# Attention head and FFT on one core: positions split 32 by 64, two filter pieces per TensorE visit

## The chip, the core and the metric

The kernel runs on one core of one Trainium2 chip. The metric is device time in microseconds (us), the median of three runs. The core's engines each follow their own list of instructions and wait for each other by semaphores: TensorE (PE in the profile, PEld for its weight loads), VectorE (DVE), ScalarE (ACT), GpSimd (POOL) and SyncE (SP). The last two mostly issue DMA transfers here.

## What is computed

Two independent results stand side by side in the output. `A` is attention with 16 query heads of 28 dimensions and one shared key and value head over 2048 positions. `B` is a filter in the frequency domain: a real two-dimensional FFT over positions (2048) and features (448), a product with a complex weight, and the way back.

```python
q = (x @ wq).reshape(B, S, H, Dh).transpose(0, 2, 1, 3)     # S 2048, H 16, Dh 28
k, v = x @ wk, x @ wv                                       # one head
p = softmax(einsum("bhqd,bkd->bhqk", q, k) * Dh ** -0.5)
a = einsum("bhqk,bkd->bhqd", p, v).transpose(0, 2, 1, 3).reshape(B, S, H * Dh) @ wo
X = rfft2(x_b, axes=(-2, -1)) * (w_r + 1j * w_i)            # 2048 x 225
b = irfft2(X, s=(S, D), axes=(-2, -1))
out = concatenate([a, b], axis=-1)
```

## The kernel before

The program has a head, a main loop and an end.

**Head.** The queries are projected in 16 groups: four chunks `c` of 512 positions by four groups `g` of 128 columns. Keys and values ride along in spare columns of the query weights. Numbers are split into a rounded part and a remainder (`xh`, `xl`, `wqh`, `wql`), so a group takes 11 matmuls (`proj`, line 367). ScalarE evacuates the result from PSUM into `qraw` and VectorE reduces its largest absolute value (`evac`, lines 371 and 372). The groups of chunks 1 to 3 are counted `n` = 0 to 11 below, group `n` being chunk `1 + n // 4`.

Between the groups stands the first stage of the filter's FFT. The 2048 positions of `B` come in eight pieces `q` of 256. For each piece VectorE folds the features (`fft1_fold`, lines 133 to 142: eight additions and subtractions, the first two over the halves of the 64 positions of a column, which makes a first radix-2 step); TensorE transforms the features (`fft1_a`, line 158, 64 small matmuls, ScalarE evacuating to `a`); TensorE transforms along positions (`fft1_b`, line 177, 16 matmuls of 64 by 64); the result `bs` is evacuated by ScalarE (pieces 0 to 5) or VectorE (6 and 7) and stored by SyncE to the DRAM tensor `t1`. Positions are split 64 by 32: 64 in this stage, 32 in the second. One piece is handled per slot: `slots` names the groups `n` = 3, 5, 6, 8, 9, 10 behind which a piece's `fft1_a` stands, with the `fft1_b` of the piece before it. Pieces 6 and 7 follow the last group, and the last `fft1_b` stands in the main loop, as unit `F` of `PLAN`.

Behind the projections come the keys and values. `fetch` copies seven four-row strips of `qraw` into `kf` rows 0 to 27 for the keys (by SyncE, one half of the positions at a time) and seven into rows 32 to 59 for the values (by GpSimd). `keys(h)` casts a half of the keys into `ka` (line 284, by ScalarE for half 0, VectorE for half 1), takes the remainder `kl` (line 288), and three DMAs copy these to three other row groups of `ka` (line 290). Half 1 is made at the very end of the head. The values are turned by 16 TensorE transposes (line 509) into one PSUM bank, which VectorE copies to `vs` (line 512). Also in the head: the largest query and key norms give a bound on the scores (`key_max` line 387, `terms`, `shift` line 299, `cmax`, `bits`), and `build_q` makes the first query tile `qa`, whose four row groups are filled by VectorE, ScalarE, SyncE and GpSimd (`copy_q`, lines 211 to 214).

In the head TensorE follows the order of the code. VectorE and ScalarE are ordered by the framework's scheduler, by the code's order and what is ready, and `behind` pins a few instructions behind others.

**Main loop.** 256 steps: 16 query tiles of (chunk, group) by 16 key tiles of 128. Per step, four score matmuls (line 929), their exponentials on ScalarE (line 864; those with `k` or `e` in `PLAN` are kept apart, lines 935, 940 and 954), and the output matmuls with `vs` (line 875). `PLAN` spreads over these steps the rest of the filter: units `A` and `B` (second FFT stage, the product with the weights, and its way back), `Z` (the first stage's way back), and `W` (output projection). All engines' orders are written out there: a host-side count of clocks in the code decides where waiting VectorE work goes. The PSUM banks are taken from a queue `free`.

**End.** The last output projection, and a slow path under a condition that these inputs do not meet.

## Time and profile before

| | |
|---|---|
| median of three runs | 633.81 us (633.77 to 633.99) |
| the profiled execution | 634.43 us |
| its span, first to last instruction | 632.6 us |
| TensorE, weight loads, VectorE, ScalarE busy | 627.0, 377.8, 440.0, 547.3 us |
| first projection behind the loads | 4.43 us |
| first score matmul (start of the main loop) | 69.22 us |
| granted TensorE clock | 1.000 |

All predicted times follow from the profiled execution's span; what lies outside it is 634.43 - 632.6 = 1.8 us. In a row of the timeline stand start, time taken, engine, line, operation, output and inputs, sizes, and how many equal instructions were merged. A matmul's record runs from its start to its modelled end, longer than the distance to the next start.

### The profile page before, as it was taken

How to read it: one execution, taken by the hardware profiler on the slowest of the kernel's cores; microseconds unless marked ns; L12 is line 12 of the kernel's file. 1: busy time of each engine (PE TensorE's matmuls, PEld its weight loads, DVE VectorE, ACT ScalarE, POOL GpSimd, SP SyncE). 2: the span in 40 equal slices, each digit the busy share in tenths (PEclk: the TensorE clock that was granted, in tenths of full speed). 3: DMA queues.
4: the chain of work that ended last, by engine and by line, in shares of the span. 5: the costliest groups of instructions: out<-in, count | busy, mean ns of one | idle time of the engine just before them, and what ended most of it. 6: DMA issues, size and time to landing. Idle time of an engine off the chain costs nothing. (4 is left out here: it accounts for less than half of the span.)

```text
span 632.6 us, 12167 instructions
## 1 busy us (share of the span) xinstructions
PE 627.0 (99%) x4436; PEld 377.8 (60%) x4436; DVE 440.0 (70%) x792; ACT 547.3 (87%) x985; POOL 61.2 (10%) x118
## 2 busy tenths in 40 slices
PE   9999999999999999999999999999999999999997
PEld 7877645656565655746555665565566565555555
DVE  5999648779999943866766845277687764467653
ACT  5655999999999998988889989999989989989992
POOL 3021311011213110000110100001010100000000
PEclk9999999999999999999999999999999999999999
DMA  8865773446456623226340413034152413030011
GB/s 249 295 175 163 235 173 99 115 132 180 121 152 144 155 59 74 67 65 187 77 106 18 125 36 82 16 83 147 35 129 60 105 53 88 16 82 11 20 31 61
DMA packets 37891, 66.74 MB, mean 106 GB/s; under 512 B 8009, under 2 KB 22746, under 8 KB 36860
## 3 DMA queue, kind: packets, MB, share of 16 engines
q1 hardware_dynamic: 32608, 52.50, 29.8%
q0 software_dynamic: 4640, 12.48, 7.9%
q8 instruction: 36, 0.59, 0.4%
q10 hardware_dynamic: 576, 0.92, 0.4%
q14 instruction: 31, 0.25, 0.1%
HBM read 29.81 MB, written 17.87 MB: 75 GB/s over the span
## 5 line engine op out<-in xcount | busy, mean ns | idle before, releaser
L864 ACT ACTIVATE p<-s 128x512 f32<-128x512 f32 x392 | 216.6, 636 | 24.9 <-PE s L929 23.9
L929 PE MATMUL s<-qa,ka 128*128 128x512 f32 x736 | 222.4, 402 | 0.0
L929 PEld LDWEIGHTS s<-qa,ka 128*128 128x128 f32 x736 | 134.7, 188 | 58.1 <-issue 26.0
L875 PE MATMUL s<-p,vs 128*32 128x512 f32 x1144 | 141.6, 595 | 0.0
L935 DVE COPY k<-s 128x512 f32<-128x512 f32 x119 | 78.2, 685 | 68.6 <-PE s L929 68.3
L954 ACT ACTIVATE k<-k 128x1024 f32<-128x1024 f32 x80 | 83.4, 1140 | 0.0
L864 ACT ACTIVATE qraw<-s 128x512 f32<-128x512 f32 x136 | 78.0, 648 | 2.3 <-PE s L929 2.3
L875 PEld LDWEIGHTS s<-p,vs 128*32 128x32 f32 x1144 | 34.5, 109 | 75.9 <-issue 69.1
L864 ACT ACTIVATE p<-po 128x512 f32<-128x512 f32 x88 | 56.0, 636 | 6.5 <-PE po L929 6.5
L929 PE MATMUL po<-qa,ka 128*128 128x512 f32 x151 | 60.9, 404 | 0.0
L929 PE MATMUL sx<-qa,ka 128*128 128x512 f32 x137 | 55.2, 403 | 0.0
L875 PE MATMUL s<-qraw,vs 128*32 128x512 f32 x424 | 54.8, 594 | 0.0
L875 PE MATMUL s<-k,vs 128*32 128x512 f32 x352 | 46.0, 594 | 0.0
L864 ACT ACTIVATE p<-sx 128x512 f32<-128x512 f32 x64 | 41.3, 645 | 3.0 <-PE sx L929 2.9
L749 POOL DMA_DIRECT2D ol<-ol x36 | 18.0, 507 | 228.0 <-DVE ol L772 155.8
L879 DVE STREAM_TRANSPOSE osb<-s 128x512 f32<-128x512 f32 x15 | 10.7, 716 | 38.9 <-PE s L875 38.8
L929 PEld LDWEIGHTS po<-qa,ka 128*128 128x128 f32 x151 | 28.4, 188 | 13.5 <-issue 6.7
L929 PEld LDWEIGHTS sx<-qa,ka 128*128 128x128 f32 x137 | 25.8, 188 | 11.0 <-issue 4.2
L875 PEld LDWEIGHTS s<-qraw,vs 128*32 128x32 f32 x424 | 13.2, 110 | 29.9 <-issue 28.7
L875 PEld LDWEIGHTS s<-k,vs 128*32 128x32 f32 x352 | 10.8, 110 | 24.9 <-issue 24.6
L864 ACT ACTIVATE qraw<-sx 128x512 f32<-128x512 f32 x35 | 22.7, 649 | 2.0 <-PE sx L929 2.0
L935 DVE COPY p<-s 128x512 f32<-128x512 f32 x37 | 24.1, 682 | 0.0
(263 smaller groups left out, 936.4 us busy)
## 6 DMA issues: line engine op xcount, KB each, us to landing
qa<-qa SPq DMA_DIRECT2D x15, 512.0 KB
raw<-xa SPq DMA_DIRECT2D x16, 256.0 KB
xb<-xb SPq DMA_DIRECT2D x8, 512.0 KB
qa<-qh SPq DMA_DIRECT2D x64, 64.0 KB
qa<-ql SPq DMA_DIRECT2D x60, 64.0 KB
t<-bs SPq DMA_DIRECT2D x16, 225.0 KB
wr<-wr POOLq DMA_DIRECT2D x16, 225.0 KB, 4.0
wi<-wi POOLq DMA_DIRECT2D x16, 225.0 KB, 5.2
```

Of the source, the lines that this page charges most:

```text
L749: nc.gpsimd.dma_start(ol[c][o, g].bitcast(F32), ol[c][r, 0].bitcast(F32))
L864: nc.scalar.activation(tiles[-1][:, h % 2], sc, AF.Exp, scale=SCALE)
L875: mm(po[c, g][32 * i:32 * i + 32], vs[:, kc], ps[i // 2][:, i % 2], start=(n == 1), stop=(n == 16))
L879: nc.vector.transpose(o, po[c, g])
L929: begun.append(mm(sc, ka[:, kc * 128:(kc + 1) * 128], qa[c, g][:, h], start=True, stop=True))
L935: nc.vector.tensor_copy(keep[i][h // 2][:, h % 2], sc)
L954: nc.scalar.activation(p, p, AF.Exp, scale=SCALE)
```

## The change

Seven parts, all but the last two in the head:

1. **Positions are split 32 by 64.** The first FFT stage transforms 32 positions, the second 64. The fold loses its first two instructions (the step over halves) and ends in the tile it began in (`xb`), from which TensorE then reads; so a piece's `xb` is free for the next load only behind its `fft1_a`. `t1` is `[64, 64, DF]`, and a second-stage tile is loaded by two DMAs of 64 partitions instead of four of 32. The constants `fw`, `fi`, `g1`, `g2` and the order of the weights follow; the sizes of the matmuls stay.
2. **Two pieces per visit.** `slots` is gone. `fft1_a` and `fft1_b` take two pieces: `a(0, 1)` behind group 4; `b(0, 1)`, `a(2, 3)` behind 7; `b(2, 3)`, `a(4, 5)` behind 10; `b(4, 5)`, `a(6, 7)`, `b(6, 7)` behind 11.
3. **The last `fft1_b` moves from the main loop into the head** (`F` leaves `PLAN`).
4. **The values are transposed on VectorE.** GpSimd fetches 28 strips of 512 positions into `vt` (7 values by 4 rows for each chunk), and one VectorE transpose in 32 by 32 blocks writes `vs`. TensorE's transposes and the evacuation go.
5. **The positions of the keys are permuted** to fit this: a key tile of 128 now takes 32 positions from each of the four chunks. So each half of `keys` fills 64 columns of every key tile, and its three DMAs move pieces of 64 elements. Half 1 is made behind group 10's `b(2, 3)`, by ScalarE.
6. **VectorE's and ScalarE's order is written out** from group 4 on; most `behind` calls are gone.
7. The order of the first `free` banks differs, and the output is put together on the host by the new split.

```diff
@@ head @@
+            ctx.enter_context(tc.manual_schedule(engines={mybir.EngineType.DVE, mybir.EngineType.Activation}))
+            group(4)
+            fft1_a(0, 1)
+            fft1_fold(2)
+            fft1_fold(3)
+            parts_of(3)
+            for j in range(NK):
+                split_x(*xs[3], 3, j)
+            group(5)
+            keys(0)
+            group(6)
+            fft1_fold(4)
+            group(7)
+            for v in range(3):
+                fetch_v(range(7, 14), v)
+            fft1_b(0, 1)
+            fft1_a(2, 3)
+            fft1_fold(5)
+            group(8)
+            group(9)
+            fetch(range(7), halves[1])
+            nc.vector.tensor_reduce(qm, qmx[:, 0:2], axis=AX.X, op=ALU.max)
+            fft1_fold(6)
+            group(10)
+            terms(0, 1)
+            fft1_fold(7)
+            fetch_v(range(7, 12), 3)
+            fft1_b(2, 3)
+            keys(1)
+            fft1_a(4, 5)
+            shift(0, 1)
+            qf, qh, ql = build_q(0, 0, True)
+            group(11)
+            terms(1, NC)
...
+        fetch_v(range(12, 14), 3)
+        copy_q(0, 1, qf, ql, nc.scalar)
+        fft1_b(4, 5)
+        copy_q(1, 1, qf, ql, nc.scalar)
+        fft1_a(6, 7)
+        for i in (2, 3):
+            copy_q(i, 1, qf, ql, nc.scalar)
         shift(1, NC)
-        top = nc.vector.tensor_reduce(cmax, cvec, axis=AX.X, op=ALU.max)
+        nc.vector.tensor_reduce(cmax, cvec, axis=AX.X, op=ALU.max)
...
+        fft1_b(6, 7)
...
-        pv = bank().rearrange("p (b d) -> p b d", b=16)
-        for b in range(16):
-            nc.tensor.transpose(pv[:, b], kf[32:64, b * 128:(b + 1) * 128], ident[32:64, 32:64])
-        fft1_out(6, pb6, bound)
-        fft1_a_out(7, 1, pa7)
-        nc.vector.tensor_copy(vs, pv)
-        keys(1, nc.vector.tensor_copy)
+        nc.vector.transpose(vs.rearrange("p t d -> p (t d)"), vt)
@@ fft1_fold @@
-            f = ff[q] = fp.tile([113, 4, 4, 2, 32], F32, name="f", tag="wi")
-            xv = x.rearrange("p k (j h m) -> p k j h m", h=2, m=32)
-            for h, op in enumerate((ALU.add, ALU.subtract)):
-                nc.vector.tensor_tensor(f[:, :, :, h], xv[:, :, :, 0], xv[:, :, :, 1], op=op)
...
+        f = fp.tile([113, 4, 256], F32, name="f", tag="wi")
+        nc.vector.tensor_tensor(f[:, 0:2], x[:, 0::2], x[:, 1::2], op=ALU.add)
+        nc.vector.tensor_tensor(f[:, 2:4], x[:, 0::2], x[:, 1::2], op=ALU.subtract)
+        nc.vector.tensor_tensor(x[:, 0], f[:, 0], f[:, 1], op=ALU.add)
+        nc.vector.tensor_tensor(x[:, 1], f[:, 0], f[:, 1], op=ALU.subtract)
+        nc.vector.tensor_tensor(x[:, 2], f[:, 2], f[:, 3], op=ALU.subtract)
+        nc.vector.tensor_tensor(x[:, 3], f[:, 2], f[:, 3], op=ALU.add)
@@ keys @@
+            src = kf[:, hs].rearrange("p (s t j) -> p s t j", s=2, j=32)
+            high = ka[:32].rearrange("p (t s j) -> p s t j", s=NC, j=32)[:, 2 * h:2 * h + 2]
+            nc.scalar.activation(high, src, AF.Copy)
...
+            kt = ka.rearrange("p (t x) -> p t x", t=16)[:, :, 64 * h:64 * h + 64]
+            low = kl.rearrange("p (t x) -> p t x", t=16)
+            for p, src in ((1, kt[:32]), (2, low), (3, low)):
+                nc.sync.dma_start(kt[32 * p:32 * p + 32].bitcast(F32), src.bitcast(F32))
@@ second stage @@
-            for l in range(2):
-                p = (r * 2 + l) * 32
-                ld = b2["last", q] = nc.sync.dma_start(b[p:p + 32].bitcast(F32), t1v[r, l][:, 4 * q:4 * q + 4])
-                behind(ld, begun[-1])
+            ld = b2["last", q] = nc.sync.dma_start(b[64 * r:64 * r + 64].bitcast(F32), t1v[r][:, 4 * q:4 * q + 4])
+            behind(ld, begun[-1])
```

Where the order moves, rows of the programs tell more. First TensorE between two groups of projections. Before, behind group 8, it does the fourth piece's first pass (L158) and the third piece's second pass (L177):

```order
L367 MATMUL s_87<-xh,wql 128x512
L158 MATMUL s_88<-cs_259,f 32x113 x4
...
L158 MATMUL s_89<-cs_259,f 32x112 x4
L177 MATMUL pbb<-a,fw 64x225 x2
L177 MATMUL po<-a,fw 64x225 x2
...
L367 MATMUL s_90<-xh,wqh 128x512
```

After the change, behind group 7 (the names are PSUM banks, `pbb` and `po` two more of them; L172 is the second pass, L155 the first):

```order
L369 MATMUL s_88<-xh,wql 128x512
L172 MATMUL pbb<-a,fw 64x225 x2
L172 MATMUL po<-a,fw 64x225 x2
...
L172 MATMUL s_89<-a,fw 64x225 x2
L172 MATMUL s_90<-a,fw 64x225 x2
L155 MATMUL s_85<-cs_260,xb 32x113 x4
...
L155 MATMUL s_88<-cs_260,xb 32x112 x4
L369 MATMUL s_89<-xh,wqh 128x512
```

Two second passes come first and two first passes behind them, and the next projection stands behind all four. Next TensorE at the end of the head and the first scores. Before:

```order
L498 MATMUL s_90<-sel_292,cmax 1x4 x4
L158 MATMUL s_85<-cs_259,f 32x113 x4
...
L509 MATMUL s_87<-ident,kf 128x32 x16
L929 MATMUL s_90<-qa,ka 128x512
...
L929 MATMUL s_85<-qa,ka 128x512
L177 MATMUL pbb<-a,fw 64x225 x2
L177 MATMUL po<-a,fw 64x225 x2
...
L875 MATMUL s_88<-k,vs 32x512 x4
```

And after:

```order
L301 MATMUL s_89<-prod,blk 128x12
L172 MATMUL pbb<-a,fw 64x225 x2
...
L172 MATMUL s_86<-a,fw 64x225 x2
L503 MATMUL s_90<-sel_291,cmax 1x4 x4
L917 MATMUL s_89<-qa,ka 128x512
L917 MATMUL s_87<-qa,ka 128x512
L917 MATMUL s_88<-qa,ka 128x512
L917 MATMUL s_85<-qa,ka 128x512
...
L863 MATMUL s_88<-k,vs 32x512 x4
```

The transposes and the second pass behind the first scores are gone, and two second passes stand ahead of the bound's matmuls and the scores. Last VectorE ahead of the main loop. Before, from the bound's input on:

```order
L494 TENSOR_REDUCE cmax<-cvec 128x4
L213 CAST qa<-qh 32x512 x2
L499 TENSOR_REDUCE bits<-s_90 1x1
L213 CAST qa<-qh 32x512 x2
L187 COPY bs<-s_88 128x450
L187 COPY bs<-s_89 128x450
L512 COPY vs<-s_87 128x512
L287 CAST ka<-kf 32x1024
L288 TENSOR_TENSOR kl<-kf,ka 32x1024
L187 COPY bs<-pbb 128x450
L187 COPY bs<-po 128x450
```

And after:

```order
L288 TENSOR_TENSOR kl<-kf,ka 32x2x16x32
L302 COPY cvec<-s_87 128x4
L232 TENSOR_SCALAR ql<-qraw,mask,cvec 128x512
...
L205 CAST qa<-qh 32x512 x4
L302 COPY cvec<-s_89 128x4x3
L499 TENSOR_REDUCE cmax<-cvec 128x4
L182 COPY bs<-pbb 128x450
...
L182 COPY bs<-s_86 128x450
L504 TENSOR_REDUCE bits<-s_90 1x1
L505 STREAM_TRANSPOSE vs<-vt 128x512
```

The remainder of the keys' second half (`kl`) has moved ahead of the first query tile, the four evacuations of the last two pieces stand together, and the transpose of the values closes the list. In the main loop the rows of TensorE and ScalarE read as before, with other bank numbers.

More of the change, by code (lines that the diff above doesn't have):

```diff
@@ L160, in fft1_a_mm, with fft1_b @@
         return pa
[L162 to L167 removed]
+    def fft1_b(*qs):
+        for i, q in enumerate(qs):
+            fft1_out(q, fft1_mm(q, [pair_of(bank()) for _ in range(2)] if i else None))
+            fft1_load(q + 4, (1,))
     def fft1_mm(q, pb=None):
@@ L479, with group @@
-            fetched = fetch(range(12, 14), slice(1536, S), nc.gpsimd)
-        behind(copy_q(0, 1, qf, ql, nc.scalar), last)
-        for p in range(2):
-            last = fft1_a_out(6, p, fft1_a_mm(6, p))
+            def group(n):
+                c, g = 1 + n // 4, n % 4
+                pq = pq1[g] if c == 1 else bank()
+                for j in range(1 if c == 1 else 0, NK):
+                    proj(pq, *xs[c], g, j)
+                if n == 10:
+                    key_max()
+                evac(c, g, pq)
@@ new lines @@
+            for n in range(4):
+                group(n)
+                if n == 0:
+                    parts_of(2)
+                    for j in range(NK):
+                        split_x(*xs[2], 2, j)
+                        xr[3, j] = raw(t["xa"][3, :, j], nc.sync)
+                    fft1_fold(1)
+                if n == 1:
+                    fetch(range(7), halves[0])
+            ctx.enter_context(tc.manual_schedule(engines={mybir.EngineType.DVE, mybir.EngineType.Activation}))
+            group(4)
@@ L495 @@
-        pb6 = fft1_mm(6, [pair_of(bank()) for _ in range(2)])
+        nc.vector.tensor_reduce(cmax, cvec, axis=AX.X, op=ALU.max)
         pb3 = bank()
+        fft1_b(6, 7)
         for g in range(NG):
             mm(pb3[0:1, 4 * g:4 * g + 4], cmax[:, g:g + 1], sel4, start=True, stop=True)
-        bound = nc.vector.tensor_reduce(bits, pb3[0:1, 0:16], axis=AX.X, op=ALU.max)
-        for i in range(4):
-            behind(copy_q(i, 0, qf, qh, nc.vector), top if i < 2 else bound)
-        for p in range(2):
-            behind(copy_q(2 + p, 1, qf, ql, nc.scalar), last)
```

182 lines of the change are left out of this document (57 added, 125 removed).

## The prediction

> **What bounds the kernel now.** I read the page first, then the busy time by stretches, the waits, and the head's instructions in order of time.
>
> ```profile
> span 632.6 us, 12167 instructions
> PE 627.0 (99%) x4436; PEld 377.8 (60%) x4436; DVE 440.0 (70%) x792; ACT 547.3 (87%) x985; POOL 61.2 (10%) x118
> ```
>
> TensorE is busy all the time, but a matmul's record overlaps the next one's, so 99% proves little. What counts is the distance between starts. The next view gives the stretch, then the busy time of TensorE, its weight loads, VectorE and ScalarE.
>
> ```profile
> 40.00:50.00 10.00, 10.00 (x119) 7.71 (x112) 9.96 (x20) 5.19 (x10) 1.54 (x4) 1.00 0.60 163
> 69.00:80.00 11.00, 11.00 (x77) 6.02 (x79) 5.39 (x9) 10.18 (x21) 0.20 (x1) 1.00 0.78 242
> 80.00:90.00 10.00, 9.92 (x55) 5.55 (x48) 3.51 (x6) 10.00 (x22) 0.43 (x1) 1.00 0.59 140
> ```
>
> In the head VectorE is as full as TensorE (9.96 of 10); behind it, from 69 to 90, ScalarE is. The list of TensorE's own waits from 20 to 70 has one entry, the 0.25 for VectorE that stands in a row below. ScalarE's list from 69 to 96 has one too (us in total, times, longest):
>
> ```profile
> ACT k L940 <- PE s L929: 0.9, 1, 0.9
> ```
>
> So the head runs at TensorE's pace, and the first 26 us of the main loop at ScalarE's: after its wait for the first scores it waits for nothing. **The end of the head is the first score's start, at 69.22**, and what moves it moves the end.
>
> **The price of a visit.** A visit is FFT work between projections. The columns are start, time, engine, line, operation.
>
> ```profile
> 20.46 0.39 PE L367 MATMUL po<-xh,wqh 128*128 128x512 f32 x1
> 24.99 0.39 PE L367 MATMUL s<-xh,wql 128*128 128x512 f32 x1
> 25.31 1.76 PE L158 MATMUL s<-cs,f 113*32 113x113 f32 x64
> 27.00 0.50 PE L367 MATMUL s<-xh,wqh 128*128 128x512 f32 x1
> 33.91 0.41 PE L177 MATMUL pbb<-a,fw 64*64 64x225 f32 x2
> 34.34 0.36 PE L177 MATMUL pbb<-a,fw 64*64 64x225 f32 x2
> 34.53 0.36 PE L177 MATMUL pbb<-a,fw 64*64 64x225 f32 x2
> 34.83 0.50 PE L367 MATMUL s<-xh,wqh 128*128 128x512 f32 x1
> 35.17 0.40 PE L367 MATMUL s<-xl,wqh 128*128 128x512 f32 x1
> 56.01 0.50 PE L387 MATMUL s<-qm,sel 128*128 128x1 f32 x4
> 56.44 1.76 PE L158 MATMUL s<-cs,f 113*32 113x113 f32 x64
> ```
>
> And from the view of one line, the shortest, median and longest of A's matmuls in ns:
>
> ```profile
> L158 PE MATMUL s<-cs,f x512: 257/259/284, 25.3 to 67.9; 113*32 113x112 f32 x86, 113*32 113x113 f32 x85
> ```
>
> I call the two passes of the FFT's first stage A (line 158, 64 matmuls a piece) and B (line 177, 16 matmuls). Projections start 0.227 apart: 20 steps from 20.46 to 24.99 take 4.53. Into A takes 0.32 (24.99 to 25.31). A's 64 matmuls end at 25.31 + 1.76 = 27.07, the last of 0.26 starts at 26.81: 1.50 from first to last start, and 0.19 to what follows (27.00). They are 16 sets of four row groups, so a further A joins at the distance of two sets, 1.50/15 = 0.10. B has its last pair at 34.55, 0.02 behind the row of 34.53, so it runs 0.64 from 33.91; a further B joins at 0.19 (34.34, 34.53); to a projection it takes 0.28. The first projection behind a visit takes 0.34 rather than 0.227 (34.83, 35.17), and those behind it a hundredth more for a while: I add 0.15 a visit. Not in the trace: projection to B (I take A's 0.32; the ends are 0.19, as from A, and 0.43, as from a score in the rows below, 69.22 + 2.24 - 0.50 = 70.96 to 71.39), and B to A (0.28, as to a projection; ends 0.19 and 0.32).
>
> **The head after, from 24.99.** Group 4: 11 projections, 2.50. Visit 1 (A, A): 0.32 + 1.50 + 0.10 + 1.50 + 0.19 = 3.61. Groups 5 to 7: 32 x 0.227 + 0.15 = 7.41. Visit 2 (B, B, A, A): 0.32 + (0.64 + 0.19 + 0.64) + 0.28 + 3.10 + 0.19 = 5.36. Groups 8 to 10: 7.41. Visit 3: the same 5.36; the key maximum makes 0.32 into 0.65 (one projection's 0.22 before it, 0.43 from 56.01 to 56.44); the shift adds 0.32. That is 6.01. Group 11: 10 x 0.227 + 0.15 = 2.42. For the last visit the rows of before are:
>
> ```profile
> 64.70 0.39 PE L299 MATMUL s<-prod,blk 128*128 128x12 f32 x2
> 65.02 0.99 PE L177 MATMUL s<-a,fw 64*64 64x225 f32 x16
> 66.26 0.32 PE L498 MATMUL s<-sel,cmax 128*1 128x4 f32 x7 [0.25 <-DVE cmax L494]
> 68.11 1.18 PE L509 MATMUL s<-ident,kf 32*128 32x32 f32 x16
> 69.22 2.24 PE L929 MATMUL s<-qa,ka 128*128 128x512 f32 x8
> 71.39 0.41 PE L177 MATMUL pbb<-a,fw 64*64 64x225 f32 x2
> 72.31 1.06 PE L875 MATMUL s<-k,vs 128*32 128x512 f32 x8
> ```
>
> After, it is visit 2's 5.36, the shift 0.32 (64.70 to 65.02), two more B 1.47, 0.28 out, the bound's matmuls 0.18, 0.15 to the score: 7.76. The transposes (68.11 to 69.22) are gone, and the wait at 66.26 is covered by the two B. The sum is 2.50 + 3.61 + 7.41 + 5.36 + 7.41 + 6.01 + 2.42 + 7.76 = 42.48, and **the first score starts at 67.47 instead of 69.22: 1.75 earlier**. In parts: transposes -1.1, wait -0.3, last B moved in +0.8, junctions the rest, some -1.1. With the unseen junctions at their ends it is 67.1 to 67.8.
>
> **The last B leaves the main loop** (0.92, 71.39 to 72.31). I cost that at nothing:
>
> ```profile
> 69.82 4.03 ACT L940 ACTIVATE k<-s 128x512 f32<-128x512 f32 x8 [0.94 <-PE s L929]
> 73.84 0.60 ACT L864 ACTIVATE p<-s 128x512 f32<-128x512 f32 x1
> ```
>
> ScalarE takes 4.03 for the first eight scores and goes on without a gap; its order there is unchanged, so it comes 1.75 earlier and no more. TensorE would reach the next scores earlier and wait. If TensorE were the limit there, it would be another 0.9.
>
> **Do the operands come in time?** VectorE loses two of eight instructions per fold. Groups of instructions, with busy time, mean ns and idle time before them:
>
> ```profile
> L133 DVE TENSOR_TENSOR f<-xb 113x512 f32<-113x512 f32 x14 | 9.1, 681 | 0.0
> 67.93 1.13 DVE L187 COPY bs<-s 128x450 f32<-128x450 f32 x2
> L371 ACT ACTIVATE qraw<-s 128x512 f32<-128x512 f32 x9 | 5.4, 598 | 11.9 <-PE s L367 11.9
> L372 DVE TENSOR_REDUCE qmx<-qraw 128x1 f32<-128x512 f32 x11 | 7.5, 678 | 0.0
> ```
>
> Per fold two of 0.6 to 0.68 go (four of the long form become two), 10 us over eight folds. That pays for the written order. There VectorE stands at the reduction of group 9 until its last projection (24.99 + 2.50 + 3.61 + 7.41 + 5.36 = 43.87, the start of group 8, + 5.0 = 48.9), its end (0.39) and its evacuation (0.6) are through, 49.9. Queued behind are that reduction (0.7) and folds 6 and 7 (2 x 2.6, with group 10's reduction and the first bound between them): done by about 56.7. TensorE wants fold 6 at visit 4's first A, 59.71 + 2.1 = 61.8. Cover 5 us; if it is gone, TensorE waits for the excess. The key maximum in visit 3 wants the reduction at 51.3: cover 0.7.
>
> Behind the first score: B 6 starts at 65.4, so VectorE's four copies run from 66.4 (0.57 each by the row, two in 1.13) to 68.7; the bound and the values' transpose, at the 716 of this row, end by 69.6:
>
> ```profile
> L879 DVE STREAM_TRANSPOSE osb<-s 128x512 f32<-128x512 f32 x15 | 10.7, 716 | 38.9 <-PE s L875 38.8
> ```
>
> The first output matmuls need four exponentials, 67.47 + 0.60 + 2.02 = 70.1. Cover 0.5. The fourth to sixth scores wait for banks until 68.1 to 68.9, ScalarE wants them from 69.6 on.
>
> **The keys** are the one new demand: key tiles now mix both halves of the keys, so the first score needs the second half, which before was needed only by the ninth tile.
>
> ```profile
> 55.32 4.57 SPq L281 DMA_DIRECT2D kf<-qraw  x7
> 78.44 1.77 SPq L599 DMA_DIRECT2D b<-t  x4
> 82.52 0.40 DVE L617 CAST bh<-b 128x450 fp32r<-128x450 f32 x1 [7.30 <-DMA b<-t]
> L284 ACT ACTIVATE ka<-kf 32x1024 fp32r<-32x1024 f32 x1 | 1.0, 1042 | 0.0
> L288 DVE TENSOR_TENSOR kl<-kf,ka 32x1024 fp32r<-32x1024 f32 x1 | 1.2, 1206 | 0.0
> wi<-wi POOLq DMA_DIRECT2D x16, 225.0 KB, 5.2
> qa<-ql POOLq DMA_DIRECT2D x4, 64.0 KB, 3.9
> L214 POOL DMA_DIRECT2D qa<-ql x4 | 2.0, 507 | 0.0
> ```
>
> SyncE has stores and loads of visit 2 ahead, long issued by then. Four of the seven fetches (4.57 for seven, 0.65 each) need group 8 alone, the last three leave by 49.9 + 2.0 = 51.9 and land 2.3 later (as the loads: issued by 80.21, used at 82.52), 54.2. ScalarE has the four evacuations of visit 3's B ahead (the last matmul of that B starts at 53.4, three more than 0.5 each behind it), until 55.0; the cast ends at 56.0. VectorE's low part, behind fold 7, ends at 57.9; its two issues behind the stores of visit 3 (some 0.65 each) end by 59.6. Landing 2.3 to 5.2 later: 61.9 to 64.8. Cover 2.7 us or more. In an unkind reading of the loads, whose 4 x 128 pieces took 4.1 in all, each key copy of 512 pieces takes 4.1 and they go one by one: 56.0 + 12.3 = 68.3, 0.8 late. I take the first, since the loads' 4.1 (78.44 to 82.52) is mostly issue (1.77) and landing (2.3). Behind the keys on SyncE four query copies issue until 62.2, and land by 67.4 even at 5.2. On POOL's queue a fetch of group 11's values (evacuated by 59.71 + 0.39 + 0.6 = 60.7) stands ahead of the other four: at 0.507 each they issue from 61.2 to 63.2, and at 3.9 the first lands at 65.1, the last, which the fourth score wants at 68.1, at 66.6. The last value fetch, behind them, lands by 67.6 at 3.9; the transpose starts at 68.9.
>
> The pieces of these copies are now 256 B, where they were 4096 B. No row has such a piece. The Trainium skill, "DMA: Bandwidth & Descriptors", Specifications, says that below 512 B a transfer leaves line rate, since the engine reads, modifies and writes; its section "Why small descriptors are slow (HBM only)" says that copies inside SBUF do not suffer so. By the second the sum above stands; the first is a rival, below.
>
> **The rivals.**
> - *TensorE limits the first scores after all*, and the last B counts too: 632.06 - 0.9 = 631.1. Against it: ScalarE's 10.18 and 10.00. Chance 0.12.
> - *Merging saves nothing*, because a visit's 0.32 and 0.28 are waits for ScalarE's evacuations, which merged visits meet again: then only transposes, wait and B are left, 1.75 - 1.1 = 0.65, 633.2. Against it: ScalarE stood idle for 11.9 us before its evacuations, waiting for TensorE (the row of line 371), not the other way round. Chance 0.10.
> - *The written order stalls*: an instruction that waits on VectorE or ScalarE holds all behind it, as the 7.30 at 82.52 shows. Some 1 us lost at the smallest covers (0.5 at the values' transpose, 0.7 at the key maximum) gives 633.0. Chance 0.18.
> - *Slower: the second half of the keys is late.* It costs from 67.47 on, makes the kernel slower by 0.2% from 69.22 + 1.27 = 70.5 on, which is at 4.8 us for each of the three copies, one by one. At twice the loads' 4.1, which is what the skill's 512 B rule would come to if it held here, 56.0 + 24.6 = 80.6: 11 us later than before, 645. Chance 0.07.
>
> **How the numbers follow.** The profiled execution took 634.43 with a span of 632.6; the median of the runs shown is 633.81, 0.62 less. 634.43 - 1.75 = 632.7 on that footing, 633.81 - 1.75 = 632.06 as a median. The forecast, 631.7 to 632.5, has 0.53. The range has to take in the first rival and most of the stalls: 630.8 to 633.4. Faster by over 0.2% (below 632.5, about what a measurement can tell): the forecast, the first rival and a little of the stalls, 0.69. Slower (above 635.1): the keys and the worst stalls, 0.08. The rest, 0.23, is the same.
>
> **What would show it.** Right: the first score near 67.5; three visits between projections, the second and third with no wait of TensorE; about 0.1 between two A of a visit; ScalarE's first exponential 0.6 behind the first score and no gap until some 24 us later; no L509 rows. Wrong: a wait of TensorE at the first score for key copies, at group 11 for folds or evacuations, or at the first output matmul for the values; or a main loop that is shorter or longer than 563.4 from first score to end by more than 0.5.

## The result, and the profile after

The changed kernel takes 632.50 us (median of 22 executions, 631.53 to 634.32) where the kernel before takes 634.25 on the same chips: a ratio of 0.9973, with a 95% interval of 0.9967 to 0.9979. That is 1.75 us or 0.27% faster; the prediction was 632.06 and 1.75 us. All ratios leave out executions in a disturbed state of the chip, which the cores' granted clocks show.

The page of the profiled execution (633.24 us) begins so:

```profile
span 631.5 us, 12130 instructions
PE 625.5 (99%) x4420; PEld 377.6 (60%) x4420; DVE 430.2 (68%) x775; ACT 547.2 (87%) x986; POOL 67.4 (11%) x132
```

VectorE has 9.8 us less to do than before (440.0), ScalarE the same (547.3). TensorE's rows in order of time show the visits (line 369 is a projection, 155 is A, 172 is B, 917 a score, 863 an output matmul):

```profile
25.61 0.39 PE L369 MATMUL s<-xh,wql 128*128 128x512 f32 x1
...
28.11 0.39 PE L369 MATMUL s<-xh,wql 128*128 128x512 f32 x1
28.43 3.30 PE L155 MATMUL s<-cs,xb 113*32 113x113 f32 x128
31.66 0.50 PE L369 MATMUL s<-xh,wqh 128*128 128x512 f32 x1
...
39.07 0.39 PE L369 MATMUL s<-xh,wql 128*128 128x512 f32 x1
...
40.20 0.94 PE L172 MATMUL s<-a,fw 64*64 64x225 f32 x16
41.07 3.30 PE L155 MATMUL s<-cs,xb 113*32 113x113 f32 x128
44.30 0.50 PE L369 MATMUL s<-xh,wqh 128*128 128x512 f32 x1
...
51.69 0.39 PE L369 MATMUL s<-xh,wql 128*128 128x512 f32 x1
...
57.50 0.48 PE L369 MATMUL s<-xh,wqh 128*128 128x512 f32 x1
...
59.88 0.39 PE L369 MATMUL s<-xh,wql 128*128 128x512 f32 x1
...
61.87 3.30 PE L155 MATMUL s<-cs,xb 113*32 113x113 f32 x128
...
66.04 0.41 PE L172 MATMUL pbb<-a,fw 64*64 64x225 f32 x2 [0.54 <-ACT a L144]
...
68.17 2.44 PE L917 MATMUL s<-qa,ka 128*128 128x512 f32 x8
70.53 1.39 PE L863 MATMUL s<-k,vs 128*32 128x512 f32 x8
```

A visit runs from the last projection ahead of it to the first behind it. This execution began 0.62 us later than that of before (the last projection of group 3 starts at 25.61, not 24.99), so distances are compared, not times:

| piece | predicted | measured |
|---|---|---|
| group 4 | 2.50 | 2.50 |
| visit 1 (28.11 to 31.66) | 3.61 | 3.55 |
| groups 5 to 7 | 7.41 | 7.41 |
| visit 2 (39.07 to 44.30) | 5.36 | 5.23 |
| groups 8 to 10 | 7.41 | 7.39 |
| visit 3 (51.69 to 57.50) | 6.01 | 5.81 |
| group 11 | 2.42 | 2.38 |
| visit 4 (59.88 to 68.17) | 7.76 | 8.29 |
| sum, from 25.61 to the first score | 42.48 | 42.56 |

Before, the same distance was 44.23: the head is 1.67 shorter. From the first score to the end it is 631.5 - 68.17 = 563.3, as before (563.4). ScalarE's start of the main loop and its only wait between 66 and 96:

```profile
68.76 4.03 ACT L928 ACTIVATE k<-s 128x512 f32<-128x512 f32 x8
72.60 0.68 ACT L852 ACTIVATE p<-s 128x512 f32<-128x512 f32 x1
```
```profile
ACT p L852 <- PE s L917: 0.5, 1, 0.5
```

TensorE's one new wait is the 0.54 at 66.04: the last visit's B waits for ScalarE's evacuation of the last A. TensorE's rows do not say why ScalarE was late. VectorE's and then ScalarE's rows do:

```profile
52.75 0.69 DVE L129 TENSOR_TENSOR f<-xb 113x512 f32<-113x512 f32 x1 [1.62 <-DMA xb<-xb]
...
58.96 1.21 DVE L288 TENSOR_TENSOR kl<-kf,ka 32x1024 fp32r<-32x1024 f32 x1
...
60.28 0.55 DVE L232 TENSOR_SCALAR ql<-qraw,mask,cvec 128x512 f32<-128x512 f32 x1
```
```profile
60.86 0.63 ACT L229 ACTIVATE qh<-ql 128x512 fp32r<-128x512 f32 x1 [2.41 <-DVE ql L232]
...
65.44 1.86 ACT L144 ACTIVATE a<-s 128x450 f32<-128x450 f32 x4
67.33 1.28 ACT L203 ACTIVATE qa<-ql 32x512 fp32r<-32x512 f32 x2
```

Fold 6 waits 1.62 for its piece of the input. SyncE's rows say when the load of a piece left, first before (piece 6), then after (pieces 6 and 7):

```profile
42.26 0.62 SPq L120 DMA_DIRECT2D xb<-xb  x1
```
```profile
46.93 1.10 SPq L120 DMA_DIRECT2D xb<-xb  x2
```

The buffer is now free only behind the first A of visit 2, which ends by 42.8 (half of the 3.30 that starts at 41.07, and its last matmul's end). The other 4 us lie in SyncE's own order, in which this load stands behind that visit's stores and small loads; no run here moves it ahead of them. Fold 7 and the low part of the keys stand behind fold 6 on VectorE, and the first query's shift (line 232) behind those. ScalarE comes to that query's cast in its written order and waits 2.41 for the shift, with the evacuation of group 11 and six more copies behind it. When the first score's result is there (68.76), ScalarE has been done with its copies for 0.15 us (67.33 + 1.28 = 68.61).

The other change is in the transfers. From the view by stretches, first before, then after; the last two columns are the share of the 16 DMA engines and GB/s:

```profile
65.00:70.00 5.00, 4.75 (x108) 3.93 (x108) 4.65 (x13) 3.96 (x8) 3.14 (x7) 1.00 0.78 212
```
```profile
65.00:70.00 5.00, 4.44 (x57) 2.55 (x50) 3.22 (x9) 4.78 (x10) 2.55 (x5) 1.00 0.92 258
```

At the end of the head the DMA engines are now busier. In this execution every copy came in time; in some of the experiments the last query copy does not.

### The profile page after: what moved, and what is told of

Read it like the earlier page. It is cut to its first block, busy times and chain, and to the rows that moved or that the text cites. A ratio compares the mean times of both kernels' runs of the same rounds, so it can differ in the third digit from the quotient of the medians.

```text
span 631.5 us, 12130 instructions
## 1 busy us (share of the span) xinstructions
PE 625.5 (99%) x4420; PEld 377.6 (60%) x4420; DVE 430.2 (68%) x775; ACT 547.2 (87%) x986; POOL 67.4 (11%) x132
## 2 busy tenths in 40 slices
DMA packets 40931, 66.71 MB, mean 106 GB/s; under 512 B 11189, under 2 KB 25926, under 8 KB 39904
```

## The experiments

In all of them the start of visit 1's A is the common mark, called V (28.43 after). "Score" and "exp" are the distances from V to the first score and to ScalarE's first exponential in the profiled execution, "rest" is from that exponential to the end. The ratio weighs every execution that it counts and lies near that of the means, so a few late ones raise it above what the median suggests.

| kernel | median, us | ratio to before, 95% | score | exp | rest |
|---|---|---|---|---|---|
| changed kernel | 632.50 | 0.9973 (0.9967 to 0.9979) | 39.74 | 40.33 | 562.7 |
| the same again | 632.26 | 0.9973 (0.9961 to 0.9984) | 38.95 | 39.54 | 563.2 |
| transposes added | 633.53 | 0.9988 (0.9979 to 0.9997) | 40.47 | 41.05 | 563.1 |
| visits taken apart | 634.26 | 0.9998 (0.9989 to 1.0008) | 40.66 | 41.24 | 563.2 |
| fold 7 later | 632.11 | 0.9970 (0.9958 to 0.9981) | 39.00 | 39.59 | 562.9 |
| last B back | 633.05 | 0.9988 (0.9976 to 1.0000) | 38.70 | 40.03 | 563.6 |
| fold 7 later, last B back | 633.34 | 0.9993 (0.9977 to 1.0010) | 38.19 | 38.86 | 567.1 |
| fold 7 later, two B back | 633.51 | 1.0001 (0.9989 to 1.0013) | 37.90 | 38.86 | 565.3 |
| both, low keys on GpSimd's queue | 632.30 | 0.9988 (0.9969 to 1.0006) | 38.20 | 38.86 | 563.8 |
| both, query copies on VectorE | 632.35 | 0.9972 (0.9961 to 0.9982) | 38.46 | 39.05 | 564.1 |
| fold 7 later, low keys on GpSimd's queue | 631.68 | 0.9968 (0.9955 to 0.9980) | 38.95 | 39.54 | 562.6 |
| the same again | 631.84 | 0.9965 (0.9951 to 0.9978) | 38.95 | 39.54 | 562.6 |

Before's profiled execution has 44.50 from its first A (one group earlier) to the first exponential and 562.8 for the rest.

### The changed kernel again

> The changed kernel itself, unedited, on the chip of this call, so that the edits below are compared with it and not only with the kernel before. Both theories: ratio to the kernel before 0.9973, as measured.

The ratio was 0.9973. Its profile differs from the first one: fold 6 waited 0.80 for its input instead of 1.62, the last B did not wait at all, and the first score stood 0.79 nearer to V. So the stall is there in some executions and not in others, with the time of one load. But here the fourth score came late. TensorE's rows, then SyncE's issues:

```profile
66.71 0.97 PE L917 MATMUL s<-qa,ka 128*128 128x512 f32 x3
68.47 1.40 PE L917 MATMUL s<-qa,ka 128*128 128x512 f32 x5 [0.79 <-ACT k L928]
```
```profile
60.76 4.04 SPq L206 DMA_DIRECT2D qa<-qh  x4
```

The four query copies took 4.04 to issue (2.50 in the first execution), and by the trace's semaphore events the last part of the last one landed at 68.33, 0.14 before the fourth score. The row names ScalarE, but in three profiled executions the fourth score starts 0.13 to 0.14 behind that landing (68.33 to 68.47 here, 68.69 to 68.82 and 67.55 to 67.69 in two kernels below), so the copy is the likely cause. ScalarE had three scores in hand, so only 0.2 us was lost.

### Sixteen transposes on TensorE again

```
         fft1_b(6, 7)
+        pv = pb3.rearrange("p (b d) -> p b d", b=16)
+        for b in range(16):
+            nc.tensor.transpose(pv[:, b], kf[:, b * 128:(b + 1) * 128], ident[:32, :32])
```

> The changed kernel with 16 transposes of 32 by 128 on TensorE put back behind the last B visit, as many as the change took out; their result is read by nobody, the values still come from VectorE. Theory 1: the first score is later by their whole stream, 1.1 us, and so is the end: ratio to the kernel before 0.9990. Rival (the head's end is set by ScalarE's or VectorE's list, which TensorE waits for anyway, and the gain came from VectorE's shorter folds): 0.3 us or less, ratio 0.9973 to 0.9978.

```profile
66.86 1.18 PE L504 MATMUL s<-ident,kf 32*128 32x32 f32 x16
67.97 0.34 PE L506 MATMUL s<-sel,cmax 128*1 128x4 f32 x8
```

They hold the stream for 1.11, and the time rose by 0.0015 in the ratio, some 0.95 us. The first theory holds: what is added to TensorE ahead of the first score arrives at the end.

### The first three visits taken apart

```
             group(4)
-            fft1_a(0, 1)
+            fft1_a(0)
...
             group(5)
+            fft1_a(1)
...
             group(6)
             fft1_fold(4)
+            fft1_b(0)
+            fft1_a(2)
             group(7)
...
-            fft1_b(0, 1)
-            fft1_a(2, 3)
+            fft1_b_bank(1)
+            fft1_a(3)
```

and in the same way `b(2)`, `a(4)` behind group 9 and `b(3)`, `a(5)` behind group 10 (`fft1_b_bank` is `fft1_b` with its results in two score banks, as the second piece of a visit has them).

> The changed kernel with its first three visits taken apart: one A, or one B and one A, behind each of groups 4, 5, 6, 7, 9 and 10, as many passes as before but six visits for three (the last visit stays). Theory 1 (what merging saves is the way into and out of a visit, 0.32 and 0.19 to 0.28, and two matmul groups' hand-over): 1.2 us later, ratio to the kernel before 0.9992. Rival (the way in and out is a wait that merged visits meet again, so merging saves nothing): the same as the changed kernel, 0.9973. In between, 0.9980 to 0.9986, would mean that half of it comes back.

It was 634.26, as slow as before the change. No row of TensorE shows a wait between 25 and 70. The first single visit:

```profile
27.16 0.39 PE L373 MATMUL s<-xh,wql 128*128 128x512 f32 x1
27.48 1.76 PE L155 MATMUL s<-cs,xb 113*32 113x113 f32 x64
29.16 0.50 PE L373 MATMUL s<-xh,wqh 128*128 128x512 f32 x1
```

It takes 2.00 (27.16 to 29.16), so two take 4.00 where the merged visit takes 3.55. In all it came to 40.66 from V to the first score, 1.71 more than the 38.95 of the changed kernel without the stall, for three visits more: 0.57 a visit. The rival that merging saves nothing is out, and the saving is larger than the 1.2 expected.

### VectorE's relief alone

```
-            xv = x.rearrange("p k (j h m) -> p k j h m", h=2, m=32)
-            for h, op in enumerate((ALU.add, ALU.subtract)):
-                nc.vector.tensor_tensor(f[:, :, :, h], xv[:, :, :, 0], xv[:, :, :, 1], op=op)
-            y = f.rearrange("p k j h m -> p k (j h m)")
-            nc.vector.tensor_tensor(e2, y[:, 0::2], y[:, 1::2], op=ALU.add)
-            fold_end[q] = nc.vector.tensor_tensor(o2, y[:, 0::2], y[:, 1::2], op=ALU.subtract)
+            nc.vector.tensor_tensor(e2, e2, o2, op=ALU.add)
+            fold_end[q] = nc.vector.tensor_tensor(o2, o2, e2, op=ALU.subtract)
```

> The kernel before with six VectorE instructions a fold instead of eight: the two that form sums and differences of neighbouring halves are left out, so the FFT is computed of other data; everything else stays, TensorE's order and the loads too. Theory 1 (VectorE is not what the head waits for, but for the 0.25 at the bound): 0.3 us faster or less, ratio 0.9995 to 1.0. Rival (most of the change's gain comes from VectorE's 10 us): 1.0 to 1.7 faster, ratio 0.9973 to 0.9984.

634.30 against 634.17, a ratio of 1.0004 (0.9995 to 1.0012). The wait at the bound went (from its first A the first score came 0.32 earlier), and that is all; a VectorE that was busy for 9.96 of 10 us was not what the head waited for.

### Fold 7 behind the query's split

```
             terms(0, 1)
-            fft1_fold(7)
...
             qf, qh, ql = build_q(0, 0, True)
+            fft1_fold(7)
```

> The changed kernel with VectorE's six instructions of fold 7 moved behind the low part of the keys, the first query's shift and its split; nothing else in any engine's order. Theory (the 0.54 that TensorE waits before the last B visit is the end of a chain: fold 6 waits for its load, fold 7 stands ahead of the query's split, ScalarE's in-order list waits 2.41 for that split with its evacuations behind it): the query's split comes some 2.5 us earlier, the wait goes, 0.5 to 0.6 us faster than the changed kernel, ratio to the kernel before 0.9964. Rival (ScalarE's list is full between 60 and 67 anyway): the wait stays, 0.9973. Against the theory: fold 7 then ends near 61.6, its A starts near 63.6, cover 2 us.

The last B starts without a wait, and ScalarE has 0.69 to spare ahead of its first exponential. TensorE's row, then ScalarE's:

```profile
64.91 0.41 PE L172 MATMUL pbb<-a,fw 64*64 64x225 f32 x2
```
```profile
57.96 0.63 ACT L229 ACTIVATE qh<-ql 128x512 fp32r<-128x512 f32 x1 [0.43 <-DVE ql L232]
...
67.45 4.03 ACT L928 ACTIVATE k<-s 128x512 f32<-128x512 f32 x8 [0.69 <-issue]
```

The cast comes with a wait of 0.43, not 2.41, although fold 6 still waited 1.19 for its load. The kernels that leave fold 7 in its place bear the chain out from the other side. There the last B's wait follows fold 6's: 0.80 for the load gave no wait, 1.24 gave 0.17 (transposes added), 1.46 gave 0.38 (last B back, below), 1.62 gave 0.54. What exceeds some 1.08 arrives at TensorE. By that the 1.19 here would have cost TensorE only 0.11, so what this profile shows is the cast's shorter wait (it was 2.06 in the second execution of the changed kernel, behind a load wait of 0.80), not the loss of 0.54 itself. In time the kernel is 0.4 us below the changed one, inside the interval: the stall is in one of the two profiled executions of the changed kernel, and the second one, without it, has the same distance to the first score (38.95 to 39.00).

### The last B back in the main loop

```
-PLAN = 2 * ["eeee"] + [...
+PLAN = ["eeee"] + ["eeeeF"] + [...
...
-        fft1_b(6, 7)
+        fft1_b(6)
+        bank(), bank()
...
+    todo = {"F": [(fft1_b, 7)], ...
```

> The changed kernel with its last B pass (16 matmuls, piece 7) put back into the main loop, behind the second step's scores, as before the change. Theory 1 (TensorE sets the head's length, ScalarE sets the first 26 us of the main loop): the head loses the second B of its last visit, some 0.8 us, and the main loop takes it in for nothing: ratio to the kernel before 0.9960, some 631.7 where before is 634.25. Rival (TensorE sets the main loop's start too): the 0.9 only moves, ratio 0.9973 as for the changed kernel, main loop from first score to end 0.9 longer. The wait of 0.54 for ScalarE at the last B visit stays in both.

(`bank(), bank()` takes two banks from the queue as the B would have, so that the later order stays.) Both expectations missed: 0.9988, slower than the changed kernel by some 0.9 us, though the intervals just overlap. The first score did come early, 1.04 nearer to V than in the first execution of the changed kernel, but ScalarE did not:

```profile
66.67 1.28 ACT L203 ACTIVATE qa<-ql 32x512 fp32r<-32x512 f32 x2
67.98 4.03 ACT L930 ACTIVATE k<-s 128x512 f32<-128x512 f32 x8
```

The first score started at 66.65, the first exponential at 67.98, right behind the last query copy in ScalarE's list. From V that is 0.30 earlier, not 1.04. In the changed kernel TensorE and ScalarE end the head within 0.2 us of each other, so a shorter TensorE list alone gains little. Why the kernel became slower is not shown: its rest is 0.9 longer than in the changed kernel, and only 0.1 of that falls in the first 24 us of ScalarE's main loop. The small gain led to the next two.

### Both edits, and a second B

The two diffs above together:

> The changed kernel with both edits: fold 7 behind the query's split, and the last B (piece 7) in the main loop. Theory 2 (at the end of the head ScalarE's list is as late as TensorE's: with the last B back alone the first score came 1.04 earlier against the start of the first visit, the first exponential only 0.30, since ScalarE's copies ended just before it; with fold 7 later alone ScalarE had 0.69 to spare): now both come early, and the first exponential starts some 0.65 earlier than with fold 7 later alone, 38.9 behind the start of the first visit instead of 39.6; the B costs 0.1 in the main loop. 0.5 faster than fold 7 later alone, ratio 0.9956 to 0.9962. Rival (the B passes through to the end wherever it stands): no faster than fold 7 later alone, 0.9965 to 0.997.

Now both lists are early: the first exponential is at 38.86 from V, as forecast. And yet the ratio was 0.9993 where 0.9956 to 0.9962 was expected, with 4 of 12 executions above 635. The profiled one is among those. TensorE's rows, ScalarE's ninth exponential, SyncE's issues, and the stretches (the third number from the end is TensorE's granted clock):

```profile
65.85 1.06 PE L919 MATMUL s<-qa,ka 128*128 128x512 f32 x3
68.82 1.81 PE L919 MATMUL s<-qa,ka 128*128 128x512 f32 x5 [1.91 <-DMA qa<-qh]
70.56 0.64 PE L172 MATMUL pbb<-a,fw 64*64 64x225 f32 x2
```
```profile
74.15 0.60 ACT L854 ACTIVATE p<-s 128x512 f32<-128x512 f32 x1 [2.26 <-PE s L919]
```
```profile
60.70 3.86 SPq L206 DMA_DIRECT2D qa<-qh  x4
```
```profile
66.00:69.60 3.60, 1.69 (x7) 1.01 (x7) 1.62 (x4) 2.34 (x5) 0.02 (x1) 1.00 1.01 283
69.60:73.00 3.40, 3.40 (x23) 1.31 (x25) 0.62 (x2) 2.29 (x5) 0.00 (x0) 0.50 0.89 314
```

The fourth score waits 1.91 for the last query copy, while the DMA engines are full (1.01), and behind that wait TensorE runs at half its clock for 3.4 us: a B matmul takes 0.64 instead of 0.41. ScalarE's ninth exponential starts 7.63 behind its first (66.52 to 74.15), where the changed kernel took 3.84 (68.76 to 72.60). That is 3.8 of the 4.4 us that the rest is longer. The Trainium skill, "TensorE: Matmul & The Clock Gate", Part 1, describes such a gate, with free-running windows of 3413 ns, and names an idle window of that length for the fall to half rate. The length and the half rate agree with this trace; but here TensorE had been idle for 1.9 of the 3.6 us ahead of it, not for a whole window.

And with the B of piece 6 out of the head too:

```
-PLAN = 2 * ["eeee"] + [...
+PLAN = ["eeeeF"] + ["eeeeF"] + [...
...
-        fft1_b(6, 7)
+        bank(), bank()
...
+    todo = {"F": [(fft1_b, 6), (fft1_b, 7)], ...
```

> As the kernel with both edits, but the B passes of pieces 6 and 7 both in the main loop, one behind each of the first two steps' scores; the head ends with the two A of its last visit. Theory 2 (ScalarE's list then ends the head: the copies of the last A and two query copies): the first score 0.7 to 0.9 earlier again, the first exponential no more than 0.1 earlier, and two B cost 0.2 to 0.4 in the main loop: the same as with both edits or up to 0.4 slower. Rival (TensorE alone sets the head): another 0.8 faster.

With two B in the main loop the first exponential stayed where it was (38.86), though the first score came another 0.29 earlier: ScalarE's list ends the head there, as forecast. The rest is 2.6 us longer than in the changed kernel (565.3 to 562.7), more than the forecast 0.2 to 0.4, and 4 of 11 executions had a mean clock of 0.997 or less.

### Taking the copies away

Two ways of getting the last query copy in earlier, both tried on the kernel with both edits. The first moves two of the key copies that stand ahead of it to another queue:

```
-                nc.sync.dma_start(kt[32 * p:32 * p + 32].bitcast(F32), src.bitcast(F32))
+                eng = nc.gpsimd if h and p > 1 else nc.sync
+                eng.dma_start(kt[32 * p:32 * p + 32].bitcast(F32), src.bitcast(F32))
```

> The kernel with both edits (fold 7 later, last B in the main loop), and the two copies of the low key half issued from GpSimd's queue instead of SyncE's, so that the four query copies behind them leave SyncE earlier. Theory 3 (what spoiled both edits together is the last query copy: its issue took 1.93 instead of 0.59 behind three key copies of 512 pieces, its last part landed at 68.69, the fourth score waited 1.91 for it, and after that wait the TensorE clock was halved for 3.4 us): the query copies issue by 61.5 and land by 66, no wait at the fourth score, no halved clock behind it in any execution, ratio to the kernel before 0.995 to 0.9965, and no executions 3 us above the others. Rival A (the wait and the halved clock come from the B in the main loop, not from the copy): the same spread as with both edits, median ratio 0.998 to 1.0. Rival B (copies of 256 B pieces are slow on either queue): the keys land late from GpSimd's queue, TensorE waits for them at the first score, slower than both edits.

A miss. The wait at the fourth score fell to 0.47 in the profiled execution, but SyncE's four issues hardly got shorter (3.45 where they took 3.86), and 2 of 12 executions were above 636. The ratio, 0.9988, lies where rival A had it. TensorE's row, then SyncE's issues:

```profile
68.06 1.40 PE L920 MATMUL s<-qa,ka 128*128 128x512 f32 x5 [0.47 <-DMA qa<-qh]
```
```profile
60.05 3.45 SPq L206 DMA_DIRECT2D qa<-qh  x4
```

One key copy's issue alone, still ahead on SyncE, took 1.88 there. So the two copies that were moved are not what makes these issues long. Nor do full DMA engines explain it by themselves: with two B back the four query copies took 2.52 to issue at a busy share of 0.93, while in the second execution of the changed kernel the last one took 2.12 of the 4.04 at a share of 0.72. What makes an issue long stays open.

The second takes the four copies out of the DMA altogether; VectorE makes them:

```
-            copy_q(i, 2, qf, qh, nc.sync)
...
+        for i in (0, 1):
+            copy_q(i, 2, qf, qh, nc.vector)
...
         nc.vector.tensor_reduce(cmax, cvec, axis=AX.X, op=ALU.max)
+        for i in (2, 3):
+            copy_q(i, 2, qf, qh, nc.vector)
```

> The kernel with fold 7 later and the last B in the main loop, and the four query copies that SyncE issued now made by VectorE (two behind its four casts, two behind the bound's reduction, 0.44 each), so that no query copy stands in SyncE's queue. Theory 3 (with the last B gone from the head, the last query copy is what TensorE waits for, and the halved clock follows that wait): no wait of TensorE at the fourth score, first exponential 38.9 behind the start of the first visit, no executions 3 us above the others, median 631.0 to 631.4, ratio to the kernel before 0.9952 to 0.9960, 0.3 to 0.6 faster than fold 7 later without the B in the main loop. Rival (the B in the main loop brings the slow executions by itself, since TensorE has no slack there): some executions at 635 and above as before, median ratio 0.997 to 0.999.

No wait for a copy, and no execution above 632.74 nor a mean clock under 0.999 in 8: with the copy went the executions above 635, and that part of the theory is borne out, as far as eight executions go (at the 6 in 24 of the two kernels above, eight without one come up one time in ten). The copies alone do not bring them either: in 45 executions of the changed kernel and of the two kernels with fold 7 later and no B in the loop, with the copies on the DMA, there was none. But the gain, 0.9952 to 0.9960, did not come. TensorE's rows, then ScalarE's:

```profile
66.03 1.42 PE L922 MATMUL s<-qa,ka 128*128 128x512 f32 x5
67.92 0.97 PE L922 MATMUL s<-qa,ka 128*128 128x512 f32 x3 [0.47 <-DVE bits L508]
68.82 0.41 PE L172 MATMUL pbb<-a,fw 64*64 64x225 f32 x2
```
```profile
66.61 4.03 ACT L933 ACTIVATE k<-s 128x512 f32<-128x512 f32 x8 [0.21 <-issue]
71.28 0.60 ACT L857 ACTIVATE p<-s 128x512 f32<-128x512 f32 x1 [0.64 <-PE s L922]
```

The sixth score now waits 0.47 for a bank that VectorE, with four more casts to do, reads late. The B and the first output matmuls stand behind the scores, and ScalarE, through with its eight exponentials, waits 0.64 for the ninth score. By these runs TensorE has just about one B of room behind the first eight scores, and only if those eight are not held up.

### Without the B in the main loop

> The kernel with fold 7 later alone, and the two copies of the low key half on GpSimd's queue. Theory 3: the last query copy lands before 66.5, the fourth score waits only for its bank; 0 to 0.3 us faster than with fold 7 later alone, ratio to the kernel before 0.9962 to 0.9970, and 0.5 slower than the kernel with the last B in the main loop as well. Rival A (the B in the main loop costs what it saves in the head): the same time as with it.

> The same kernel as the one with fold 7 later and the low key copies on GpSimd's queue, run again on the chip of this call to stand beside the kernel with the query copies on VectorE. Both theories: ratio 0.9968 as measured, no executions above 633.5.

Fold 7 later and the low keys on GpSimd's queue, the last B in the head: 631.68 and 631.84 on two chips. Its medians are the lowest here, some 2.4 us under before and 0.4 to 0.8 under the changed kernel; its ratios (0.9968, 0.9965) and that of the changed kernel (0.9973) have overlapping intervals, so the second figure is likely rather than shown, and nothing sets it apart from fold 7 later alone (0.9970). The ratio came as expected; two other forecasts missed. The last query copy landed at 67.55, not before 66.5, and in the first profile the fourth score waited for it (67.69). The kernel with the last B in the main loop as well, expected to be 0.5 faster, was slower by its ratio (0.9988). In both profiles the last B does not wait and ScalarE goes through its first eight exponentials without a gap.

## Why the prediction was right, step by step

**TensorE's stream sets the head.** Right for what was changed there: sixteen transposes put back cost 0.95 us of their 1.11, visits taken apart 1.6 to 2.0 (by the ratios and by the medians), VectorE's relief alone gave nothing. But TensorE leads by little. In the profiled execution ScalarE's list ended 0.15 ahead of the first exponential; the last query copy landed 1.9 ahead of the fourth score there (67.05, by its events, to 68.97), and in the second execution 0.8 later than TensorE could have used it. The prediction named TensorE as the bound and did not say how far behind the next two were.

**The visits.** Right in kind, and priced too high. The groups between are met to 0.04; the visits are 0.06, 0.13 and 0.20 shorter than worked out, and the fourth, without its wait, 0.25 (from 7.76 to 7.51 in the second execution of the changed kernel). What the trace of before did not show was taken near the dear end: B to A at 0.28 (with B's own 0.64 the distance is 40.20 to 41.07, 0.87, so 0.23). "Junctions -1.1" was mis-sized: in an execution without the stall the head is 44.23 - 41.78 = 2.45 shorter (V of the second execution less the 2.82 from group 3's last projection, 27.75 - 2.82 = 24.93, to 66.71); with transposes -1.11, wait -0.25 and the last B +0.88 the junctions are -1.97.

**Do the operands come in time.** This step failed, by one wait. "Done by about 56.7" was 58.96 for fold 7 (58.34 without the 0.62 by which this execution began later), since fold 6's input came 1.62 late: I had counted VectorE's own queue and TensorE's need of the folds ("cover 5 us", and A did not wait for a fold), but not when the load of piece 6 leaves, which is now behind an A and then behind that visit's stores on SyncE (46.93, where it was 42.26); and not that behind the folds stands the query's split, for which ScalarE's list stops. The rival "the written order stalls" named the kind and not the place: it looked for it at the values' transpose and the key maximum, where the covers held (the transpose ended at 70.04, the first output matmul started at 70.53). The 0.78 that the stall cost in the profiled execution (8.29 for visit 4 against 7.51) and the visits' cheaper price nearly cancel: 42.56 measured, 42.48 forecast. That the sum came out so close is luck.

**The last B at nothing.** Right: 563.3 from first score to end where 563.4 was expected, and against before the first 23.7 us of ScalarE's main loop are 0.10 shorter. The inference that the B could then stay outside for nothing too is what the first experiment on it refuted: the first 24 us of ScalarE's main loop, 23.65 in the changed kernel, took 23.76 with the last B back and 24.40 where the sixth score was held up.

**The keys.** Right. The last key copy was issued by 61.5 (59.6 forecast) and all had landed by 63.8 (61.9 to 64.8), 4.4 ahead of the first score. Each copy of 512 pieces of 256 B took 2.9 to 4.0 from the start of its issue to its last part. The trace's records of single pieces add the price: one of 256 B took 21.4 ns on its DMA engine (mean of the 1536 of these three copies), one of 4096 B in the same three copies before 189 (mean of 96), so the same bytes took 1.8 times as long. Spread over the 16 engines that is 0.69 against 0.38 us a copy (512 x 21.4 and 32 x 189, over 16), little beside issue and landing. The Trainium skill's two sections on small pieces, cited in the prediction, go apart here: the loss of line rate, as in the first, shows in the pieces, and that copies inside SBUF do not suffer, as in the second, holds here only for what the whole copy takes. The first names no factor; the prediction's twice the whole 4.1 did not come. What the prediction did not weigh is the sum of the transfers at the end of the head (0.92 of the DMA engines from 65 to 70, 0.78 before): the query copies, given "by 67.4 even at 5.2", landed at 67.05 in one execution and 68.33 in the next. Whether it is this sum that delays them, and which of the moved transfers matters, was not tried.

**The time.** 632.06 was forecast as a median and 632.50 measured, at the edge of the forecast's 631.7 to 632.5, since before itself came out at 634.25 and not 633.81; the difference is the 1.75 that was forecast. Which of the two waits (the stall, or the late copy) an execution meets decides 0.2 to 0.8 us of it, so the agreement to a few hundredths in the difference is partly luck.

What stays open: the rest from first exponential to end varies by 0.6 us between kernels with the same main loop (562.6 to 563.2), and no run was made on that.

## What to carry to other kernels

When several engines reach a stage's end together, write down for each how long before the end its list is done: the step that is cut gains no more than the distance to the second. Where a buffer's last reader moves from an early engine to a late one, follow the load that refills it: what stands ahead of it in its queue, then everything queued behind the instruction that waits for that load, on every engine whose order is fixed. Work put into the slack behind another engine is free only up to the finished work that this engine has in hand: one B cost 0.1 us here at best, and 0.75 when the scores ahead of it were held up.

## What the runs showed of the hardware

- A wait of TensorE of 1.91 us inside a full stream was followed by 3.4 us at a granted clock of 0.50. Half of 3.4 us in 632 is 0.0027 of the mean clock, and executions with a mean clock of 0.997 or less were 4 of 12, 4 of 11 and 2 of 12 in the three kernels with fold 7 later, a B in the main loop and the query copies on the DMA, 1 of 11 with the B back alone, and none of the 53 of the changed kernel, of the two without a B there and of the one with the copies on VectorE. Only one such execution was profiled; for the others the cause is argued from the clock. A mean is also lowered by the end of the program: the 0.998 of the profiled execution with two B back is all from its last 2.2 us (granted clock 0.50, TensorE with nothing left to do).
- The issue of one query copy on SyncE took 0.58 to 2.12 us, 0.59 in most cases, without the busy share of the DMA engines telling them apart (0.93 where four were issued in 2.52, 0.72 during the 2.12). Four took 2.50 to 4.04 with the low keys on SyncE and 3.45 to 4.41 with these on GpSimd's queue.
- A DMA piece of 256 B between places in SBUF took 21.4 ns on its engine, one of 4096 B 189, on average over the copies of the keys' second half after and before.
- V came between 27.47 and 28.43 us after the first instruction in kernels that are the same up to there: 1 us of spread ahead of anything that was changed.
